# Seven block products in two of three d_ff groups of the gated expert for batches 0 and 1, the norm in its inputs, and a planner with one port for two engines

## The chip, the cores and the metric

One core of a Trainium2 chip runs the whole program. The metric is the device time of one execution in microseconds (us), given as the median of several runs. The engines are TensorE (PE, its weight load PEld), VectorE (DVE), ScalarE (ACT), GpSimd (POOL) and SyncE (SP, which only issues DMAs).

## The reference

The input is one attention layer (4 batches, 12 heads, 448 tokens, head size 64) and the weights of two dense layers behind it. Cut to what matters:

```
q_n, k_n = rmsnorm(q, g_q), rmsnorm(k, g_k)
x = softmax(q_n @ k_n.T / 8) @ v                     # to 1792 tokens x 768
h = x @ w_in;  y = elu(h) @ w_out                    # d_ff 2048
xn = y / sqrt(mean(y * y) + 1e-6) * rms_g
g = xn @ w_gate                                      # d_ff 1536
out = (g * sigmoid(g) * (xn @ w_val)) @ w_out2
```

All is float32. TensorE multiplies in a rounded form (fp32r), so each operand is split into a rounded high part and the difference, and a product of two 128-wide blocks takes three matmuls (high by high, high by low, low by high).

## The kernel before, in words

Everything is kept transposed: features on 128 partitions, the 448 tokens of one batch along the free side. 768 is 6 blocks, 2048 is 16 blocks, 1536 is 12 blocks. Attention goes by pairs of heads, 6 pairs to a batch, 24 in all; a pair is cut into 15 or 13 pieces (scores, softmax, transposes, product with v).

The work of the two dense layers stands in `STAGES` (line 558): the first layer for batch 0, the first for batch 1, the second for batches 0 and 1 together, the first for batches 2 and 3, the second for 2 and 3. They are called stages 1 to 5 here. `GOALS` (line 1308) says how many attention pairs are to be done by the end of each stage: 13.25, 19.75, then all 24. The main loop (line 1321 on) adds attention pieces between the steps of a stage at an even rate.

A stage goes by d_ff groups of four blocks (`NF1`, `NF2`): first the products into these four blocks, and then `acc_units` (line 1139), which multiplies them by the second matrix and adds to the result, six output blocks for each batch. In the second layer a group's first part is the gate and the value product of each block. There are three such groups.

Stages 1 to 3 are plain: `h_unit` and `gv_unit` (line 1242) make a block by `product` (line 1010) over six input blocks, 18 matmuls. Stages 4 and 5 (`FAST`, line 559) take two d_ff blocks and two batches at a time: `quad` (line 1024) gets four results by seven half-length products (`part`, three input blocks, 9 matmuls each) instead of eight. For that, `w_split` (line 612) makes the combinations of the weights (sa, sb) and `combo` (line 1048) those of the inputs: from B11, B21, B12, B22 it makes T1 to T4, and each of the seven names is split in high and low part. A set of inputs in that form fills 7 x 3 x 2 = 42 slots of `xslots`. There are 24 slots, and 18 more (`spare`) in buffers of the attention, which `late` (line 1311) adds once the last pair is done. At the end of stage 3 `combos` (line 1069) loads the spilled attention outputs of batches 2 and 3 and makes their 42 slots while TensorE does the last group's `acc_units`.

The rms norm of the second layer: `first_experts` (line 1166) puts rms_g into its output when it splits it (`y_done`, line 1172) and adds up squares; `norm` (line 1226) sums them over partitions by TensorE, takes the root on ACT and the reciprocal on DVE; the result rt is multiplied into the gate in `gv_unit` and `gv_quad` (line 1101), twice: once ahead of the tanh and once behind it.

Weights come as 768 KB chunks of six blocks. In its first use a chunk is converted to float32 by `w_convert` (line 630: two instructions on ACT or POOL, two on DVE) and, if used again, written back as `kept`; later stages load `kept`. Each is then split by `split_w` (line 603: a rounded copy, and a difference on DVE or POOL) into one of the four tiles of `r_w`; `late` adds two (`wide`).

The order of all instructions is made by `Plan` (line 34). Every operation is entered with the engines that can do it and a price on each (`copy`: DVE, ACT or POOL; `tt`: DVE or POOL; `stt`: DVE). `forward` (line 170) plays a list schedule with these prices, `backward` (line 131) makes ranks from it, and eight rounds of the two are made; the best order by its own reckoning is issued on every engine and DMA queue. An operation inside SBUF on DVE or POOL is made longer where the other engine runs too (`STRETCH`, 0.6 and 0.25 of the overlap). Buffers come in rings, and their reuse is a dependence: `r_m` has three product banks while attention runs (`phase`, line 548), `r_tp` six temporary tiles, eight after `late`.

Of the kernel before, what the change touches and what calls it, by code (L numbers as in the profile page):

```python
# [35 lines left out]
class Plan:  # L36
# [4 lines left out]
    PASSES = 8  # L41
    LAT = 0.2
# [6 lines left out]
    STRETCH = {"v": 0.6, "g": 0.25}  # L49
# [36 lines left out]
    def add(self, alts, outs, ins, lag=0.0, after=None, soon=False, dma=False):  # L86
# [24 lines left out]
        shared = not any(getattr(ap.tensor, "_space", None) == PSUM for ap in list(outs) + list(ins) if ap is not None)  # L111
        self.ops.append((alts, preds, lag, soon, dma, shared))

    def schedule(self):
# [5 lines left out]
        best, rank = None, list(range(n))  # L120
# [10 lines left out]
    def backward(self, span, start, eng, price, lat):  # L131
# [8 lines left out]
        def avail(i):  # L140
            e, is_dma = eng[i], self.ops[i][4]
            r = 0.0 if self.succ[i] else lat[i]
            for s in self.succ[i]:
                if is_dma:
                    gap = lat[i] + 0.1
                elif eng[s] == e:
                    gap = 0.06 if e != "pe" else 0.0
                else:
                    gap = lat[i] + self.LAT
                r = max(r, left[s] + gap)  # L150
            heapq.heappush(fut[e], (r, i))
# [18 lines left out]
    def forward(self, rank):  # L170
# [14 lines left out]
        port = {"v": 0.0, "g": 0.0}  # L185
# [3 lines left out]
        def avail(i):  # L189
            for e in self.ops[i][0]:  # L190
                r = 0.0
                for j in self.ops[i][1]:
                    if self.ops[j][4]:
                        f = done[j] + 0.1
                    elif eng[j] == e:
                        f = done[j] - self.ops[j][2] + (0.06 if e != "pe" else 0.0)
                    else:
                        f = done[j] + self.LAT
# [7 lines left out]
        while left:  # L206
# [23 lines left out]
            i = heapq.heappop(now[e])[1]  # L230
            alts = self.ops[i][0]
            back[e] -= alts[e][0]
            if taken[i]:
                continue
# [11 lines left out]
            if e in self.STRETCH and self.ops[i][5]:  # L246

                o = "g" if e == "v" else "v"
                price += self.STRETCH[e] * max(0.0, min(port[o], t + price) - t)
                port[e] = t + price  # L250
# [11 lines left out]
            else:  # L262
                done[i] = free[e] + self.ops[i][2]
# [31 lines left out]
def kernel(ctx: ExitStack, tc: tile.TileContext, dims, tok, qk, vr, gq, gk, wst, rmsg, ident_in, out):  # L295
# [42 lines left out]

    class Pair:
# [28 lines left out]
    def c_v1(n):  # L368
        return 0.15 + 0.00104 * n

    def c_v2(n):
        return 0.15 + 0.00052 * n

    def c_a(n):
        return 0.18 + 0.00083 * n

    def mm(o, l, r, start, stop, price=None):
        n = size(r)
        plan.add(
            {"pe": (price or max(0.108, n / 2400.0 + 0.017), lambda: T.matmul(o, l, r, start=start, stop=stop))},  # L380
            [o], [l, r] + ([] if start else [o]), lag=0.17,
        )

    def block(mms, price):
# [12 lines left out]
        plan.add({"pe": (price, go)}, list(outs.values()), list(ins.values()), lag=0.17)  # L397

    def transposes(pairs):
# [4 lines left out]
        plan.add({"pe": (0.02 + 0.11 * len(pairs), go)}, [o for o, _ in pairs], [i for _, i in pairs] + [ident], lag=0.17)  # L404

    def copy(dst, src, eng="vag"):
# [6 lines left out]
        if "a" in eng:  # L413
            alts["a"] = (c_a(n), lambda: A.activation(out=dst, in_=src, func=AF.Copy))
        if "g" in eng and not ps:
            alts["g"] = (
                0.2 + 0.00097 * n,
# [7 lines left out]
    def c_tt(a, b, n):  # L425
        return 0.2 + 0.0014 * n if two_sbuf(a, b) else c_v1(n)

    def tt(dst, a, b, op, eng="vg"):
# [4 lines left out]
        if "g" in eng and two_sbuf(a, b):  # L433
            alts["g"] = (0.25 + 0.0022 * n, lambda: G.tensor_tensor(out=dst, in0=a, in1=b, op=op))
# [18 lines left out]
    def act(dst, src, func, extra=0.0, accum=None, after=None, **kw):  # L453
        if accum is not None:
            kw["accum_out"] = accum
        plan.add(
            {"a": (c_a(size(src)) + extra, lambda: A.activation(out=dst, in_=src, func=func, **kw))},
# [3 lines left out]
    def vop(price, fn, outs, ins, after=None):  # L461
        plan.add({"v": (price, fn)}, outs, ins, after=after)

    def recip(dst, src):
        vop(0.15 + 0.00625 * size(dst), lambda: V.reciprocal(dst, src), [dst], [src])
# [30 lines left out]
    wraw = sb.tile([P, 2, 2 * WN], F32, name="wr")  # L496
    r_wr = Ring(tiles=[wraw[:, k].rearrange("p (n w) -> p n w", w=2) for k in range(2)])
    wf = wraw.rearrange("p a n -> p (a n)")
# [4 lines left out]
    tks = [tagged(1, [P, 15 * D], "tk")[0], wf[:, 0:15 * D]]  # L503
    tks += [yf[:, 7 * S:7 * S + 15 * D], yf[:, 12 * S - 15 * D:12 * S]]
    l_rw = Pair(tagged(1, [P, 1024], "rw")[0], wf[:, 1024:2048])
    l_rb = Pair(tagged(1, [P, 512], "rb")[0], wf[:, 2048:2560])
    l_qh = Pair(sb.tile([P, 1024], F32R, name="qh"), gf[:, 0:1024])
    l_ql = Pair(sb.tile([P, 1024], F32R, name="ql"), gf[:, 1024:2048])
    p_own = tagged(1, [P, 3, 2 * S], "p")[0]
    pt_own = tagged(1, [P, 2, 3, S], "pt")[0]  # L510
    l_p = Pair(p_own, tf[:, 0:6 * S].rearrange("p (a s) -> p a s", a=3))
    l_pj = Pair(tagged(1, [P, S], "pj")[0], tf[:, 6 * S:7 * S])
    l_pt = Pair(pt_own, yf[:, 0:6 * S].rearrange("p (h k s) -> p h k s", h=2, k=3))
    l_pe = Pair(tagged(1, [P, S], "pe")[0], yf[:, 6 * S:7 * S])
# [3 lines left out]
    r_sn = Ring("sn", 1, [P, NPB * 15])  # L518
# [11 lines left out]
    spare, wide = [], []  # L530
# [5 lines left out]
    for t in (l_rb.own, l_pj.own, l_pe.own, r_rv.t[0], r_rv.t[1], r_rsb.t[1]):  # L536
# [22 lines left out]
    FAST = (3, 4)  # L559
    OG = NF1 * CD // CW  # L560

    def steps_of(kind, fast):
        nums = list(one if kind == 1 else two)
        if not fast:
            return [("c", n) for n in nums]
# [871 lines left out]
```

## Time and profile before

| | us |
|---|---|
| median of 3 runs (1270.31 to 1271.68) | 1271.13 |
| the profiled execution | 1273.35 |
| its span, first to last instruction | 1271.6 |
| TensorE busy in the span (6300 matmuls) | 1231.3 |
| DVE, ACT, POOL busy | 835.1, 681.7, 919.1 |

The span is that of the profiled execution, which took 1273.35 us. Most of the program's instructions are recorded at line 319, since a wrapper issues them all, so groups go by tile names: bank is a PSUM bank, xs and late are input slots, w and late weight tiles, gbig the d_ff blocks, tbig, rsb and xf temporaries, ybig results, wr raw weights, wc converted ones. Matmul records overlap by their pipeline, so a busy time close to the length of a stretch doesn't say that the stretch is full; the count of matmuls in it says more.

### The profile page before, as it was taken

Reading aid. Unit: us, or ns where it says so; the run is one execution under the profiler, and the core shown is the slowest. Engines: PE = TensorE matmul, PEld = TensorE weight load, DVE = VectorE, ACT = ScalarE, POOL = GpSimd, SP = SyncE. Lnnn points to the kernel's source line nnn. Section 1 sums busy time; section 2 is a strip of 40 time slices with the busy share of each in tenths; the row PEclk is TensorE's granted clock in tenths of the full one; section 3 lists DMA queues with packets and bytes.
Section 4 is the critical chain, followed back from the end, with each engine's and each line's share of the span. In section 5 each row is a group of like instructions: output and inputs, shape, how many; then the busy total and the mean of one; then the engine's idle time right before and its main releaser. Section 6 shows DMA issues by size and latency. Waiting matters only on the chain.

```text
span 1271.6 us, 17832 instructions
## 1 busy us (share of the span) xinstructions
PE 1231.3 (97%) x6300; PEld 1025.9 (81%) x6300; DVE 835.1 (66%) x1276; ACT 681.7 (54%) x1328; POOL 919.1 (72%) x688
## 2 busy tenths in 40 slices
PE   4998999999999999999999999999999999999998
PEld 2556867777777877898988888999999978999997
DVE  6886888879545588764554547626354899486582
ACT  5876767676655577554554543535334754342240
POOL 3587879997766697775653569948476999798680
PEclk9998999999999999999999999999999999999999
DMA  5677676775443444664444435212121112122112
GB/s 201 190 227 260 245 247 234 240 248 156 165 131 120 124 178 160 218 202 161 156 165 128 149 94 169 88 38 75 47 66 63 38 32 73 58 63 75 38 50 87
DMA packets 62206, 173.44 MB, mean 136 GB/s; under 512 B 10654, under 2 KB 19876, under 8 KB 62116
## 3 DMA queue, kind: packets, MB, share of 16 engines
q1 hardware_dynamic: 53476, 163.31, 39.3%
q10 hardware_dynamic: 8640, 8.99, 2.5%
q8 instruction: 49, 0.80, 0.2%
q14 instruction: 41, 0.34, 0.1%
HBM read 137.11 MB, written 35.17 MB: 135 GB/s over the span
## 4 chain that ended last, share of the span: by engine, by line
PE 79%; POOL 9%; DVE 4%; DMA 3%; issue 2%; ACT 1%; SPq 0%; ACTq 0%; POOLq 0%; DVEq 0%
PE bank L319 79%; POOL w L319 2%; POOL tbig L319 1%; POOL gbig L319 1%; POOL late L319 1%; POOL wr L319 1%; POOL xs L319 1%; DVE bank L319 1%; DMA rb<-scr 1%; DVE ybig L319 1%; POOL ql L319 1%; DMA tk<-tok 0%; DMA ybig<-tok 0%; DMA wc<-kept 0%; DMA wr<-wst 0%
## 5 line engine op out<-in xcount | busy, mean ns | idle before, releaser
L319 PE MATMUL bank<-xs,w 128*128 128x448 f32 x1872 | 423.0, 371 | 1.7 <-DVE tbig L319 0.9
L319 PE MATMUL bank<-gbig,w 128*128 128x448 f32 x1872 | 408.0, 372 | 2.8 <-POOL gbig L319 2.7
L319 PEld LDWEIGHTS bank<-gbig,w 128*128 128x128 f32 x1872 | 347.8, 189 | 43.0 <-issue 7.1
L319 PEld LDWEIGHTS bank<-xs,w 128*128 128x128 f32 x1872 | 344.6, 188 | 38.2 <-issue 6.7
L319 POOL TENSOR_TENSOR w<-wc,w 128x768 fp32r<-128x768 f32 (+1 forms) x126 | 241.8, 1921 | 81.1 <-ACT w L319 75.1
L319 DVE TENSOR_REDUCE bank<-bank 128x1 f32<-128x448 f32 x168 | 99.3, 624 | 76.2 <-PE bank L319 75.8
L319 ACT ACTIVATE w<-wc 128x768 fp32r<-128x768 f32 (+1 forms) x82 | 65.2, 795 | 91.7 <-PE bank L319 85.8
L319 DVE SCALAR_TENSOR_TENSOR wc<-wc,wt 128x768 int32<-128x768 int32 x68 | 92.2, 1356 | 26.9 <-ACT wc L319 16.5
L319 POOL TENSOR_TENSOR gbig<-tbig,gbig 128x448 fp32r<-128x448 f32 x75 | 99.8, 1333 | 8.7 <-ACT gbig L319 7.4
L319 ACT ACTIVATE p<-bank,nm,rr 128x448 f32<-128x448 f32 x126 | 90.2, 720 | 27.2 <-DVE nm L319 20.6
L319 POOL TENSOR_SCALAR w<-wc 128x768 fp32r<-128x768 f32 x65 | 60.9, 938 | 57.5 <-PE bank L319 51.6
L319 ACT ACTIVATE pt<-bank 128x384 f32<-128x384 f32 (+1 forms) x161 | 68.7, 448 | 50.6 <-PE bank L319 47.8
L319 DVE TENSOR_TENSOR tbig<-bank,tbig 128x448 f32<-128x448 f32 x80 | 48.5, 617 | 57.5 <-PE bank L319 55.4
L319 POOL TENSOR_TENSOR tbig<-tbig 128x448 f32<-128x448 f32 x45 | 59.5, 1324 | 28.3 <-DVE tbig L319 27.1
L319 DVE TENSOR_TENSOR ybig<-bank,ybig 128x448 f32<-128x448 f32 x72 | 44.4, 619 | 49.0 <-PE bank L319 48.8
L319 PE MATMUL bank<-ident,p 128*128 128x128 f32 x441 | 70.6, 277 | 5.4 <-ACT p L319 3.7
L319 PEld LDWEIGHTS bank<-ident,p 128*128 128x128 f32 x441 | 53.8, 141 | 23.0 <-ACT p L319 4.3
L319 PE MATMUL bank<-xs,late 128*128 128x448 f32 x288 | 69.5, 370 | 0.4 <-DVE xs L319 0.4
L319 DVE TENSOR_SCALAR wt<-wr 128x768 uint16<-128x768 uint16 x68 | 67.7, 995 | 1.5 <-DMA wr<-wst 1.2
L319 DVE SCALAR_TENSOR_TENSOR ybig<-bank,ybig 128x448 f32<-128x448 f32 x48 | 29.8, 622 | 55.1 <-PE bank L319 55.1
L319 PE MATMUL bank<-late,w 128*128 128x448 f32 x252 | 64.6, 368 | 0.0
L319 ACT ACTIVATE wt<-wr 128x768 uint16<-128x768 uint8 x42 | 45.7, 1089 | 28.6 <-DVE wc L319 20.7
(232 smaller groups left out, 2105.1 us busy)
## 6 DMA issues: line engine op xcount, KB each, us to landing
wr<-wst SPq DMA_DIRECT2D x68, 768.0 KB
wc<-kept SPq DMA_DIRECT2D x100, 384.0 KB
kept<-wc SPq DMA_DIRECT2D x68, 384.0 KB
rw<-qk SPq DMA_DIRECT2D x21, 512.0 KB
tk<-tok SPq DMA_DIRECT2D x20, 480.0 KB
rv<-vr SPq DMA_DIRECT2D x24, 256.0 KB
out_t<-ybig SPq DMA_DIRECT2D x24, 224.0 KB
rb<-scr ACTq DMA_DIRECT2D x36, 128.0 KB
```

The source lines that it names most:

```text
L319: return lambda *a, **k: f(*[real(x) for x in a], **{n: real(x) for n, x in k.items()})
```

## The change

Of the three d_ff groups of stage 3, the first stays plain and the other two go by quads (`PLAIN`). For that the norm factor is multiplied into the inputs of batches 0 and 1 (`scale`, right behind `norm`), with a copy of the scaled block written to DRAM; `gv_unit` and `gv_quad` for these batches no longer use rt. Between the first group's products and its `acc_units`, the loop finishes attention, adds the spare slots and calls `widen`, which loads the scaled blocks again and makes T1 to T4; the splits of B11, B21 and B22 are there already. The two wide weight tiles are now the raw weight tiles, and come at the end of stage 3. The second-stage goal is 20.25 pairs, and the rest of attention is spread over the first group's eight units of stage 3. Some buffers change places: wr, p and pt become separate tiles, and pe is 512 wide, so that one copy fills both its halves in `t_bank`.

The planner has new prices, 22 rounds from ranks with noise, and one port: an operation of POOL, and one of DVE inside SBUF, begins only when the other's is over, and DVE may take another ready operation that doesn't need the port.

```diff
-    PASSES = 8
-    LAT = 0.2
+    PASSES = 22
+    SEED = 17
+    HOP = {"pe": 0.12, "v": 0.04, "a": 0.04, "g": 0.09, "sp": 0.04}
+    TAIL = {"pe": 0.0, "v": 0.085, "a": 0.11, "g": 0.04, "sp": 0.0}
+    BEHIND = {"v": 0.15, "g": 0.05}
+    SLACK = 0.1
-    STRETCH = {"v": 0.6, "g": 0.25}
...
-        best, rank = None, list(range(n))
+        noise = random.Random(self.SEED)
+        best, rank = None, [i + 40 * noise.random() for i in range(n)]
...
+            if e == "v" and self.ops[i][5] and port > t + 0.1:
+                x = min((x for x in now["v"] if not taken[x[1]] and not self.ops[x[1]][5] and t + self.ops[x[1]][0]["v"][0] <= port + self.SLACK), default=None)
...
-            if e in self.STRETCH and self.ops[i][5]:
-
-                o = "g" if e == "v" else "v"
-                price += self.STRETCH[e] * max(0.0, min(port[o], t + price) - t)
-                port[e] = t + price
+            if e == "g" or e == "v" and self.ops[i][5]:
+                if port > t:
+                    price = port - t + max(0.03, price - self.BEHIND[e])
+                port = t + price + self.TAIL[e]
...
     def c_v1(n):
-        return 0.15 + 0.00104 * n
+        return 0.064 + 0.00105 * n
...
+    def c_gt(n):
+        return 0.14 + 0.00216 * n
...
     def c_tt(a, b, n):
-        return 0.2 + 0.0014 * n if two_sbuf(a, b) else c_v1(n)
+        return c_v1(n)
...
-            alts["g"] = (0.25 + 0.0022 * n, lambda: G.tensor_tensor(out=dst, in0=a, in1=b, op=op))
+            alts["g"] = (c_gt(n), lambda: G.tensor_tensor(out=dst, in0=a, in1=b, op=op))
...
-    for t in (p_own, pt_own):
+    for t, k in ((p_own[2], 2), (pt_own[1], 3)):
         f = again(t)
-        wide.append(f[:, 0:2 * WN].rearrange("p (a n) -> p a n", a=2))
-        spare += [f[:, 2 * WN + k * S:2 * WN + (k + 1) * S] for k in range(2)]
-    r_ws = Ring(tiles=[wf[:, k * WN:(k + 1) * WN] for k in range(2)])
-    r_th = Ring(tiles=[wf[:, 2 * WN + k * S:2 * WN + (k + 1) * S] for k in range(3)] + [r_wt.t[0][:, 0:S]])
+        spare += [f[:, j * S:(j + 1) * S] for j in range(k)]
+    wide = [again(t).rearrange("p (a n) -> p a n", a=2) for t in wr]
+    r_ws = Ring(tiles=[t[:, 0:WN] for t in p_own[0:2]])
+    r_th = Ring(tiles=[pt_own[0][:, k] for k in range(3)] + [l_pj.own])
...
-    FAST = (3, 4)
+    PLAIN = (9, 9, 1, 0, 0)
...
-            copy(pe[0:64, 64:S], ps[0:64, 0:M3], "va")
-            copy(pe[64:128, 0:M3], ps[64:128, 0:M3], "va")
+            copy(pe[:, 64:S], ps[:, 0:M3], "va")
...
-    def combo(c, x):
+    def combo(c, x, ready={}):
         def sp(name, t):
-            h, l = xslots.get(), xslots.get()
-            copy(h, t)
-            tt(l, t, h, ALU.subtract)
+            if name in ready:
+                h, l = ready[name]
+            else:
+                h, l = xslots.get(), xslots.get()
+                copy(h, t)
+                tt(l, t, h, ALU.subtract)
...
         def gate(i, j, o):
-            u, th = r_tp.next(), r_th.next()
+            th = ths[i, j] = r_th.next()
+            if bs[j] < 2:
+                act(th, o, AF.Tanh, scale=0.5)
+                stt(th, th, 1.0, o, ALU.add, ALU.mult)
+                return
+            u = r_tp.next()
...
+    def widen(bs):
+        b0, b1 = bs
+        for c in range(3):
+            x = [r_tp.next() for _ in range(4)]
+            for t, (b, k) in zip(x, ((b0, c), (b0, c + 3), (b1, c), (b1, c + 3))):
+                dma(t, xsp[b, k], P * S * 4)
+            done = {n: xns[b][k] for n, b, k in (("B11", b0, c), ("B21", b0, c + 3), ("B22", b1, c + 3))}
+            combo(c, x, done)
...
-            if not fast:
-                xh, xl = xslots.get(), xslots.get()
-                act(xh, ye, AF.Copy, scale=g)
-                stt(xl, ye, g, xh, ALU.mult, ALU.subtract)
-                xns[b][e] = (xh, xl)
...
+            if not fast:
+                xns[b][e] = ye
+                return
...
+    def scale(b):
+        for e in E_ORDER:
+            ye = xns[b][e]
+            stt(ye, ye, rg[:, e:e + 1], rt[b], ALU.mult, ALU.mult)
+            xh, xl = xslots.get(), xslots.get()
+            copy(xh, ye)
+            tt(xl, ye, xh, ALU.subtract)
+            xns[b][e] = (xh, xl)
+            xsp[b, e] = tc.dram_tile([P, S], F32, name=f"xsp{b}_{e}")
+            dma(xsp[b, e], ye, P * S * 4)
+            yslots.put(ye)
...
-            u, th = r_tp.next(), r_tp.next()
-            tt(u, og, rt[b], ALU.mult)
-            act(th, u, AF.Tanh, scale=0.5)
-            stt(th, th, 1.0, u, ALU.add, ALU.mult)
-            tt(th, th, rt[b], ALU.mult)
-            ths[b] = th
+            th = ths[b] = r_tp.next()
+            act(th, og, AF.Tanh, scale=0.5)
+            stt(th, th, 1.0, og, ALU.add, ALU.mult)
...
+        fast = f0 >= plain * NF2
...
+            if f0 + NF2 == plain * NF2:
+                for x in xns[bs[1]][0:3]:
+                    for z in x:
+                        xslots.put(z)
+                yield "late"
+                widen(bs)
             yield from acc_units(bs, f0, NF2, f0 == 0, last, ob, True, o_done)
+            if f0 + NF2 == plain * NF2:
+                phase(2)
...
-    GOALS = [13.25, 19.75, 24, 24, 24]
+    GOALS = [13.25, 20.25, 24, 24, 24]
...
             for b in bs:
                 norm(b)
+                if b < 2:
+                    scale(b)
```

## Rows read from the trace of the kernel before

**Rows 1.** The page, parts 1 and 2: busy time by engine, TensorE's 40 slices.

```profile
PE 1231.3 (97%) x6300; PEld 1025.9 (81%) x6300; DVE 835.1 (66%) x1276; ACT 681.7 (54%) x1328; POOL 919.1 (72%) x688
...
PE   4998999999999999999999999999999999999998
```

**Rows 2.** Windows: stretch, length, busy us (count) by engine, granted clock, DMA share, GB/s.

```profile
0.00:30.00 30.00, 12.64 (x62) 8.25 (x62) 19.64 (x52) 15.85 (x29) 7.87 (x13) 1.00 0.60 212
...
90.00:120.00 30.00, 25.73 (x131) 18.83 (x130) 20.35 (x27) 17.14 (x28) 22.04 (x18) 0.99 0.82 275
120.00:150.00 30.00, 29.21 (x142) 23.73 (x142) 23.02 (x33) 21.67 (x44) 25.76 (x18) 0.90 0.73 248
...
270.00:300.00 30.00, 28.18 (x148) 22.30 (x149) 24.98 (x38) 18.09 (x34) 24.44 (x18) 1.00 0.68 210
...
1020.00:1050.00 30.00, 27.70 (x123) 22.99 (x122) 29.82 (x28) 16.47 (x27) 30.00 (x21) 0.94 0.13 40
...
1110.00:1140.00 30.00, 30.00 (x149) 27.57 (x148) 25.43 (x33) 12.61 (x20) 28.36 (x20) 1.00 0.17 54
1140.00:1170.00 30.00, 30.00 (x147) 27.36 (x146) 22.13 (x30) 10.93 (x17) 27.16 (x19) 1.00 0.26 80
...
560.00:765.00 205.00, 204.97 (x1055) 175.14 (x1053) 100.21 (x159) 104.58 (x184) 112.22 (x85) 1.00 0.45 146
```

**Rows 3.** Waits of TensorE, longest first: total us, times, longest us.

```profile
PE bank L319 <- DVE rr L319: 8.0, 1, 8.0
```

**Rows 4.** Timeline of TensorE, end of stage 3: start, us, group, idle before it.

```profile
765.03 29.44 PE L319 MATMUL bank<-gbig,w 128*128 128x448 f32 x144
...
799.17 1.28 PE L319 MATMUL bank<-late,late 128*128 128x448 f32 x5 [0.23 <-POOL late L319]
```

**Rows 5.** Timeline, stage 3's first products and batch 1's reciprocal.

```profile
477.08 0.89 PE L319 MATMUL bank<-xs,w 128*128 128x448 f32 x3
...
488.31 2.94 DVE L319 RECIPROCAL tbig<-tbig 128x448 f32<-128x448 f32 x1
```

**Rows 6.** Timeline, single instructions of DVE and POOL inside SBUF.

```profile
455.62 0.96 DVE L319 TENSOR_TENSOR w<-wc,w 128x768 fp32r<-128x768 f32 x1 [0.38 <-ACT w L319]
...
483.81 0.60 DVE L319 TENSOR_TENSOR gbig<-tbig,gbig 128x448 fp32r<-128x448 f32 x1
...
484.34 0.60 DVE L319 TENSOR_SCALAR wt<-wr 128x768 uint16<-128x768 uint16 x1
...
487.45 0.95 DVE L319 SCALAR_TENSOR_TENSOR wc<-wc,wt 128x768 int32<-128x768 int32 x1
...
490.61 1.84 POOL L319 TENSOR_TENSOR w<-wc,w 128x768 fp32r<-128x768 f32 x1
...
491.17 1.74 DVE L319 TENSOR_SCALAR wt<-wr 128x768 uint16<-128x768 uint16 x1
...
772.53 0.56 DVE L319 TENSOR_TENSOR wr<-wc 128x384 f32<-128x384 f32 x1 [0.21 <-DMA wc<-kept]
...
783.35 1.01 POOL L319 TENSOR_TENSOR wr<-wc,wc 128x384 f32<-128x384 f32 x1
```

**Rows 7.** Groups by form: count, busy us, mean ns, idle before and its releasers.

```profile
L319 POOL TENSOR_TENSOR w<-wc,w 128x768 fp32r<-128x768 f32 x117 | 230.6, 1972 | 80.3 <-ACT w L319 74.3 <-PE bank L319 2.5
...
L319 DVE TENSOR_TENSOR tbig<-bank,tbig 128x448 f32<-128x448 f32 x80 | 48.5, 617 | 57.5 <-PE bank L319 55.4 <-ACT tbig L319 1.6 <-issue 0.2
...
L319 DVE TENSOR_TENSOR w<-wc,w 128x768 fp32r<-128x768 f32 x19 | 27.6, 1453 | 4.8 <-ACT w L319 3.0 <-POOL w L319 1.8
```

**Rows 8.** Windows, instructions on the xs slots alone, columns as in rows 2.

```profile
477.00:493.80 16.80, 9.98 (x42) 7.51 (x42) 4.05 (x4) 1.33 (x2) 0.00 (x0) 1.00 0.34 112
```

**Rows 9.** Timeline, first and last instruction of the inputs for batches 2, 3.

```profile
755.20 0.58 ACT L319 ACTIVATE xs<-tbig 128x448 fp32r<-128x448 f32 x1
...
802.74 1.15 POOL L319 TENSOR_TENSOR late<-tbig,late 128x448 fp32r<-128x448 f32 x1 [0.69 <-ACT late L319]
```

**Rows 10.** Windows, the last second-matrix products of stage 3, columns as in rows 2.

```profile
765.00:794.50 29.50, 29.50 (x147) 27.34 (x146) 21.98 (x26) 9.07 (x17) 28.17 (x22) 1.00 0.59 174
```

More of the change, by code (lines that the diff above doesn't have):

```diff
@@ L84, in region, with add @@
         return ap.name, halves, m
-    def add(self, alts, outs, ins, lag=0.0, after=None, soon=False, dma=False):
+    def add(self, alts, outs, ins, lag=0.0, after=None, soon=False, dma=False, port=True):
         i = len(self.ops)
@@ L110, in add @@
                 self.hist[name] = keep
-        shared = not any(getattr(ap.tensor, "_space", None) == PSUM for ap in list(outs) + list(ins) if ap is not None)
+        shared = port and not any(getattr(ap.tensor, "_space", None) == PSUM for ap in list(outs) + list(ins) if ap is not None)
         self.ops.append((alts, preds, lag, soon, dma, shared))
@@ L337, in next, with grow @@
             return self.t[(self.k - 1) % len(self.t)]
+        def grow(self, more):
+            j = self.k % len(self.t)
+            self.t = list(more) + self.t[j:] + self.t[:j]
+            self.k = 0
     class Pair:
@@ L402, in go @@
                 T.transpose(o, i, ident)
-        plan.add({"pe": (0.02 + 0.11 * len(pairs), go)}, [o for o, _ in pairs], [i for _, i in pairs] + [ident], lag=0.17)
+        plan.add({"pe": (0.02 + 0.11 * len(pairs), go)}, [o for o, _ in pairs], [i for _, i in pairs] + [ident], lag=0.16)
     def copy(dst, src, eng="vag"):
@@ L455, in act, with vop @@
             kw["accum_out"] = accum
+            extra += 0.09
+        if any(hasattr(kw.get(k), "tensor") for k in ("scale", "bias")):
+            extra += 0.09
         plan.add(
-            {"a": (c_a(size(src)) + extra, lambda: A.activation(out=dst, in_=src, func=func, **kw))},
+            {"a": (c_a(size(src), in_psum(src)) + extra, lambda: A.activation(out=dst, in_=src, func=func, **kw))},
             [dst, accum], [src] + [x for x in kw.values() if hasattr(x, "tensor") and x is not accum], after=after,
         )
-    def vop(price, fn, outs, ins, after=None):
-        plan.add({"v": (price, fn)}, outs, ins, after=after)
+    def vop(price, fn, outs, ins, after=None, port=False):
+        plan.add({"v": (price, fn)}, outs, ins, after=after, port=port)
     def recip(dst, src):
-        vop(0.15 + 0.00625 * size(dst), lambda: V.reciprocal(dst, src), [dst], [src])
+        vop(0.1 + 0.00625 * size(dst), lambda: V.reciprocal(dst, src), [dst], [src])
     def dma(dst, src, nbytes, after=None, soon=False, by="sp"):
@@ L495 @@
     WN = CW * P
-    wraw = sb.tile([P, 2, 2 * WN], F32, name="wr")
-    r_wr = Ring(tiles=[wraw[:, k].rearrange("p (n w) -> p n w", w=2) for k in range(2)])
-    wf = wraw.rearrange("p a n -> p (a n)")
+    wr = tagged(2, [P, 2 * WN], "wr")
+    r_wr = Ring(tiles=[t.rearrange("p (n w) -> p n w", w=2) for t in wr])
     r_wc = Ring("wc", 3, [P, WN])
@@ L568, in steps_of @@
         for g in range(len(nums) // (nf + OG)):
+            if g < plain:
+                res += [("c", n) for n in nums[k:k + nf + OG]]
+                k += nf + OG
+                continue
             if kind == 1:
@@ L577, in steps_of @@
         return res
-    stream = [st for s, (kind, _) in enumerate(STAGES) for st in steps_of(kind, s in FAST)]
+    stream = [st for s, (kind, _) in enumerate(STAGES) for st in steps_of(kind, PLAIN[s])]
     spl_w = {}
@@ L1323 @@
         ahead = STAGES[s + 1] if s + 1 < len(STAGES) else None
-        spilled = ahead is not None and ahead[0] == 1 and ahead[1][0] >= 2
-        count = UNITS[kind] - (CD if spilled else 0)
-        rate = max(goal - pieces["n"], 0) / count
+        count = UNITS[kind] if kind == 1 else 2 * NF2 * PLAIN[s]
+        rate = max(goal - pieces["n"], 0) / max(count, 1)
         credit = 0.0
-        if s and GOALS[s - 1] >= NPAIR:
-            until(target(NPAIR) + 1)
-            phase(2)
         if kind == 2:
@@ L1334 @@
                     norm(b)
-        for step in (first_experts if kind == 1 else second_experts)(bs, s in FAST):
+        for step in first_experts(bs, s >= 3) if kind == 1 else second_experts(bs, PLAIN[s]):
+            if step == "late":
+                until(target(NPAIR) + 1)
+                late()
+                continue
             if step == "next":
-                if ahead is not None and ahead[0] == 1 and s + 1 in FAST:
-                    if not state:
-                        until(target(NPAIR) + 1)
-                        late()
+                if ahead is not None and ahead[0] == 1 and s + 1 >= 3:
+                    r_w.grow(wide)
                     combos(ahead[1])
```

130 lines of the change are left out of this document (62 added, 68 removed).

## The prediction

> **What bounds the kernel now.** The page's summary comes first: TensorE is busy for 1231.3 of 1271.6 us, the others 54 to 72%, and the slices keep TensorE at 9 from the third on [rows 1]. So a microsecond counts only if it leaves or enters TensorE's stream. Busy time hides small gaps, so I read the 30 us windows next, where the reader should compare the count of matmuls too [rows 2]. Full windows of quad products hold 147 to 149; the poor ones are those of the start (12.64 us busy of 30), of 90 to 150 us (25.73 busy in one, 0.90 of the granted clock in the other), of 270 to 300, and 1020 to 1050, with 123 matmuls where DVE and POOL are both busy all the time (29.82 and 30.00). Stage 3, which the change rewrites, is none of these: from 560 to 765 us TensorE is busy 204.97 of 205 us. The list of waits says the same: its longest, 8.0 us, belongs to the start [rows 3]. In stage 3 there is nothing to gain but matmuls.
>
> **Matmuls removed.** In one d_ff group of four blocks, plain gate and val cost 4 blocks x 2 matrices x 2 batches x 18 = 288 matmuls; four quads cost 4 x 7 x 9 = 252. Two groups change: 72 matmuls go. The second-matrix products of a group are 144 matmuls in 29.44 us [rows 4], 0.2044 us each. 72 x 0.2044 = **-14.7 us**, all on the path.
>
> **Norm moved ahead of stage 3.** Before, g alone is put into the inputs, and rt into the gate's outputs, so stage 3's products start at 477.08 while batch 1's norm is under way: the reciprocal runs from 488.31 to 491.25 [rows 5]. After, batch 1's first input needs that reciprocal, then the scaling, the rounding copy and the difference (about 0.6 each on a free DVE or ACT, 1.15 on POOL [rows 6, 9]): about 493.8. Queued behind it are six such inputs, and their spill writes on SP. Until then TensorE has batch 0's gate and val of one block, 36 matmuls, since the three product banks rotate and the next waits for batch 1; attention stays as it was. In 477 to 493.8 it ran 42 matmuls on xs [rows 8], so 6 (1.2 us) lack. Ends: 0, if the new ranks pull the chain forward, and 1.2 plus five more inputs at 1.5 us, 8.7. I take **+2**, near the low end, because 3.75 pairs of attention are still there to fill. Batch 0's norm has all of stage 2 as cover: nothing.
>
> **The T operands between groups 0 and 1.** widen makes 4 combinations and 4 splits for each of three c: 36 instructions (24 two-input, 12 copies) and 12 loads. It needs attention's buffers and batch 1's first inputs, so it waits for the last attention pair and the last plain product; its cover is group 0's 29.44 us of second-matrix products. The nearest thing in the trace is the same job for batches 2, 3: 54 such instructions, from 755.20 to 803.89, beside an equal 29.44 us, with a wait of 0.23 us at its end [rows 4, 9]. There DVE is busy 21.98 and POOL 28.17 of 29.5 us [rows 10], with no weight conversion in it. Now there are 18 fewer of these but six chunks to convert: 6 x (0.60 + 0.95) = 9.3 us of DVE [rows 6]. Ends: 0 (two thirds of the work) and 9.3, all of it uncovered. I take **+3**, a third, as the 18 left out (9 copies, and 9 differences at 1.15 on POOL) give 10.4 us of POOL back. The last group's own step to batches 2, 3 begins a few us later, since all 42 slots are held until the last quad; the same 0.23 us wait says that it just fits: inside these ends.
>
> **The quads themselves.** Per two quads (126 matmuls, 25.7 us of TensorE), unstretched durations [rows 6, 7, 9]: DVE reading PSUM 20 x 0.62 = 12.4; DVE inside SBUF, fixed, 4 chunks x (0.60 + 0.95) + 0.6 = 6.8; movable between DVE and POOL 8 half sums, 6 full and 2 half weight differences, 5 others, 14.4 on DVE (at 0.56, 0.96, 0.60) or 26.9 on POOL (1.01, 1.84, 1.15). The rows show that SBUF work of the two goes one after the other: a DVE instruction of 0.60 us, issued at 491.17 beside a POOL difference that ends at 492.45, takes 1.74 us and ends at 492.91 [rows 6]. With a share x of the movable on DVE, DVE needs 19.2 + 14.4x and the two in SBUF 33.7 - 12.5x; they meet at x = 0.54, 27.0 us, 1.3 over TensorE, 5.2 for four such pairs. Stage 5's quads by the same sum (no conversion, two rt products more per gate) need 25.6, and there 149 and 147 matmuls per 30 us run without a gap [rows 2]. So the new quads are some 5% past a load that was just carried, and a quad's weights prefetched under each group's second-matrix products take part of it. Ends 0 and 5.2 at the best split; I take **+2**. Dropped with rt: two instructions per gate and batch, off the path.
>
> By the Trainium skill (SBUF — State Buffer, Who interferes with whom) the pair of ports that VectorE and GpSimd share is an exclusive lock, held for the whole instruction. The row at 491.17 agrees; by the partial stretch that the old plan assumed (0.6 and 0.25) the two quads would need about 22 us and cost 0, by the rule 5.2.
>
> **Attention squeezed.** The last 3.75 pairs now sit in 8 units instead of 30-odd. Eight units of 36 matmuls are 58.9 us of products, 15.7 to a pair; stage 1 had 576 matmuls, 117.7 us, for 7.25 pairs, 16.2 to one. So it is stage 1's density, where a worse window (270 to 300) leaves TensorE idle for 1.8 us [rows 2]. Against that 0.5 pair moves to stage 2, which has room. I count 0 here, since the waits above already hold it.
>
> **The new plan.** All orders change: 22 passes from noisy ranks, new prices, a lock in place of stretches. Open to it are the idle times after the first 30 us: 90 to 150, 270 to 300 and 1020 to 1050 alone hold 4.3 + 0.8 + 1.8 + 23 missing matmuls (4.7) = 11.6 us [rows 2], more with the stretches like them between. A new order can lose as well. Ends -18 and +5. I take **-6**, half of the 11.6: the worst of it (1020 to 1050) is two engines contending, which the new model prices.
>
> **Sum.** -14.7 + 2 + 3 + 2 - 6 = -13.7. The profiled execution took 1273.35 us (span 1271.6); so 1259.65, and as the median of runs, 1271.13, lies 2.2 lower, **1257.4 us**.
>
> **Rivals.** *The new waits eat the gain:* norm 4, T operands 5, quads 4, plan only -3: -4.7, 1266.4. For: every engine is loaded just there. Against: 560 to 765 us has DVE at 100 of 205 us, room to work ahead. *The plan opens more:* it takes the -18 and stage 3 costs 7: -25.7, 1245.4. For: 11.6 us are visible; against: most of the rest is start-up chains over DMA. *Slower, by the port:* if the plan leaves the movable work on POOL, as it does now (117 weight differences there [rows 7], 19 on DVE in the same form), the SBUF sum per two quads is 33.7 - 12.5x. It decides once it passes 25.7 + 14.7/4 = 29.4, at x below 0.34; at x = 0.2 it is 31.2, 5.5 over, +22 in all: -14.7 + 22 + 2 + 3 - 6 = +6.3, 1277.4. Against: the old prices called DVE's difference 1.28 us for 768 columns, the new one 0.87, so work moves to DVE. That the change does nothing is out: the 72 matmuls are in the program or not.
>
> **Chances.** Forecast 0.50 (1250 to 1263), waits eating the gain 0.24 (1263 to 1271, its last bit no change), plan opening more 0.15 (1240 to 1250), port 0.11. A measurement here can tell about 0.2%, 2.5 us: faster 0.82, within it 0.07, slower 0.11. The range 1245 to 1270 leaves out the port case, and the ends of two others, about 0.2.
>
> **What would show it.** Right: 6228 matmuls; TensorE dense in the quads of stage 3, a gap of a few us or none before batch 1's first product, DVE's SBUF differences more and POOL's fewer, 1020 to 1050 fuller. Wrong: TensorE waiting on POOL w, POOL or DVE tbig in stage 3's quads (port), on xs after the reciprocal (norm), or on late tiles after group 0 (T operands) for over 5 us each; or new gaps in stages 1 and 2, where the change removes no work.

## The result, and the profile after

The changed kernel takes 1238.55 us against 1270.72 us for the one before on the same chip: ratio 0.974 (95% interval 0.9721 to 0.976), 32 us faster; one of its four executions, at 3015.5 us, was in a slow state and is left out of the ratio. The forecast was 1257.4, with a range from 1245 to 1270. The sign was right; the forecast gain of 13.7 us was less than half of the measured one. Run again beside other kernels in a later job, it took 1238.10 us (0.9744, 0.9725 to 0.9762).

The profiled execution took 1236.46 us. The page's parts 1 and 2, to be read against [rows 1]:

```profile
span 1234.7 us, 17825 instructions
...
PE 1201.6 (97%) x6228; PEld 1009.7 (82%) x6228; DVE 883.5 (72%) x1332; ACT 720.9 (58%) x1413; POOL 903.7 (73%) x651
...
PE   3999999999999999999999999999999989999998
```

TensorE runs 6228 matmuls, 72 fewer, as counted. Its idle time outside those busy 1201.6 us went from 40.3 to 33.1 us, and busy time itself fell by 29.7 us, twice the removed matmuls' 14.7. Gaps too short to show as idle, stretches at a lower granted clock (0.90 to 0.94 in [rows 2]) and the slower rhythm of the last section all count as busy. So the windows' counts have to be read. First those of the changed kernel, one long stretch and six short ones (columns as in [rows 2]):

```profile
30.00:330.00 300.00, 295.32 (x1625) 217.45 (x1625) 244.19 (x429) 242.73 (x536) 224.43 (x164) 0.99 0.71 234
...
600.00:630.00 30.00, 30.00 (x149) 27.69 (x148) 25.20 (x30) 18.68 (x29) 28.30 (x20) 1.00 0.39 134
630.00:660.00 30.00, 30.00 (x149) 27.69 (x149) 27.66 (x36) 17.42 (x25) 28.20 (x19) 1.00 0.42 152
...
690.00:720.00 30.00, 30.00 (x150) 27.79 (x149) 29.33 (x36) 18.03 (x27) 28.17 (x20) 1.00 0.47 165
720.00:750.00 30.00, 30.00 (x150) 27.80 (x149) 29.87 (x35) 18.84 (x31) 29.11 (x20) 1.00 0.54 179
...
990.00:1020.00 30.00, 25.96 (x119) 21.34 (x117) 29.55 (x28) 13.55 (x21) 29.44 (x22) 1.00 0.17 53
1020.00:1050.00 30.00, 29.61 (x147) 27.38 (x147) 29.46 (x45) 12.12 (x20) 26.01 (x18) 1.00 0.24 68
```

The same long stretch of the kernel before:

```profile
30.00:330.00 300.00, 284.27 (x1521) 207.09 (x1522) 248.14 (x418) 216.98 (x467) 246.36 (x183) 0.98 0.69 226
```

Three things are to be seen. In the first 330 us, where the change takes away no matmul, TensorE is busy for 11 us more and gets 104 matmuls further. In stage 3's quads (600 to 780 us) it runs 149 to 150 per 30 us and waits for nothing, though in the fullest of these windows (720 to 750) DVE is busy for 29.87 and POOL for 29.11 of 30 us. And the step from stage 4 to stage 5 (990 to 1020, [rows 2] had it at 1020 to 1050) is as poor as it was: 119 matmuls.

The span can be cut into three parts. Up to stage 3's first product the changed kernel:

```profile
0.00:468.84 468.84, 443.71 (x2443) 330.20 (x2444) 343.44 (x637) 349.83 (x770) 320.53 (x241) 0.99 0.64 211
```

and the kernel before:

```profile
0.00:477.08 477.08, 443.99 (x2397) 328.77 (x2397) 350.92 (x631) 322.15 (x708) 355.11 (x277) 0.99 0.61 197
```

Stage 3 begins 8.2 us earlier with 46 more matmuls done, attention that used to come later. At this stretch's 0.192 us per matmul they are some 8.8 us, so the start gained about 17 us. From there to the last 2273 matmuls, which are stages 4 and 5 in both kernels, it takes 293.7 in place of 317.2 us. Less the 8.8 us of moved attention, that is 14.7, the price of the 72 matmuls. The last 2273 take 472.2 in place of 477.3 us. These are estimates from one profiled execution of each kernel; the two spans are 36.9 us apart, the medians 32.

### The profile page after: what moved, and what is told of

Same layout as the page of the kernel before. It is cut to its first block, busy times and chain, and to the rows that moved or that the text cites. A ratio compares the mean times of both kernels' runs of the same rounds, so it can differ in the third digit from the quotient of the medians.

```text
span 1234.7 us, 17825 instructions
## 1 busy us (share of the span) xinstructions
PE 1201.6 (97%) x6228; PEld 1009.7 (82%) x6228; DVE 883.5 (72%) x1332; ACT 720.9 (58%) x1413; POOL 903.7 (73%) x651
## 4 chain that ended last, share of the span: by engine, by line
PE 88%; DVE 5%; ACT 2%; DMA 2%; issue 1%; POOL 1%; SPq 0%; ACTq 0%; DVEq 0%
PE bank L331 88%; DVE tbig L331 2%; DMA wr<-wst 1%; DVE rw L331 1%; ACT tbig L331 1%; DVE w L331 1%; DMA ybig<-tok 0%; DMA rb<-scr 0%; ACT p L331 0%; DVE bank L331 0%; POOL w L331 0%; DVE ybig L331 0%; DVE ss L331 0%; DVE ql L331 0%; DMA wc<-kept 0%
## 5 line engine op out<-in xcount | busy, mean ns | idle before, releaser
L331 PE MATMUL bank<-xs,w 128*128 128x448 f32 x1584 | 364.5, 371 | 1.8 <-DVE tbig L331 1.1
L331 PEld LDWEIGHTS bank<-xs,w 128*128 128x128 f32 x1584 | 290.6, 188 | 31.9 <-issue 7.1
L331 POOL TENSOR_TENSOR w<-wc,w 128x768 fp32r<-128x768 f32 (+1 forms) x120 | 226.8, 1892 | 54.4 <-ACT w L331 48.2
L331 PE MATMUL bank<-late,w 128*128 128x448 f32 x420 | 100.6, 366 | 0.8 <-DVE w L331 0.8
L331 ACT ACTIVATE pt<-bank 128x384 f32<-128x384 f32 (+2 forms) x175 | 75.7, 451 | 22.9 <-PE bank L331 20.6
L331 POOL TENSOR_TENSOR gbig<-tbig,gbig 128x448 fp32r<-128x448 f32 x57 | 76.9, 1354 | 13.5 <-ACT gbig L331 12.8
L331 PEld LDWEIGHTS bank<-late,w 128*128 128x128 f32 x420 | 78.8, 188 | 7.7 <-DVE w L331 1.2
L331 POOL TENSOR_TENSOR w<-p,w 128x768 fp32r<-128x768 f32 x32 | 64.5, 2017 | 20.2 <-ACT w L331 19.7
L331 POOL TENSOR_SCALAR w<-wc 128x768 fp32r<-128x768 f32 (+1 forms) x48 | 45.4, 947 | 44.4 <-PE bank L331 35.1
L331 ACT ACTIVATE tbig<-bank 128x448 f32<-128x448 f32 x78 | 42.1, 541 | 39.8 <-PE bank L331 31.9
```

The costliest lines, as they stand in the source:

```text
L331: return lambda *a, **k: f(*[real(x) for x in a], **{n: real(x) for n, x in k.items()})
```

## The experiments

All were timed in three rounds beside the kernel before, whose median lay between 1269.80 and 1270.82 us in these jobs. They answer five questions in turn.

**1. Is it the planner or the work?** plan_only is the kernel before with the new class Plan and the new prices alone; work_only is the changed kernel with the old ones.

```diff
 # plan_only: before.py, and of the change only this and the prices it uses
+    PASSES = 22
+    SEED = 17
...
+            if e == "g" or e == "v" and self.ops[i][5]:
+                if port > t:
 # work_only: the changed kernel, and this and the old prices back
+    PASSES = 8
+    STRETCH = {"v": 0.6, "g": 0.25}
```

> The work, buffers and goals of before, ordered by the new planner (prices, port, 22 noisy rounds). Theory A (the planner gave most of what the forecast missed): TensorE's gaps of the first 330 us go from some 38 us to under 12 as in the changed kernel, time 1249 to 1254 us (17 to 22 below before). Theory B (the gain beyond the matmuls comes from the work: norm in the inputs, attention squeezed, separate buffers): at most 6 below, 1264 to 1269.

Measured: 1265.48 us (0.996, 0.9944 to 0.9976), 4 below before. That is B's side.

> The changed work, buffers and goals, ordered by the old planner with its old prices and partial stretch. A: 72 matmuls are 14.7 us, the new waits of stage 3 (forecast: 7) show up here, so 1257 to 1264 us. B: most of the 32 us is kept, 1240 to 1246. If the old planner can't feed the quads at all (the port rival of the forecast): 1271 or more, with TensorE waiting on POOL's weight differences between 600 and 780 us.

Measured: 1262.48 us (0.994, 0.992 to 0.9959), 7 below before: A's side. Neither part gives the 32 us, and the two together, 12, fall far short of it. Both theories fall as they were put (the expectation for seed_101 below calls the two that are left C and D): either single orders differ by more than I had allowed, or the parts need each other. The next two changes of the planner and three of its noise ask for that.

```diff
 # search_back: the changed kernel
-    PASSES = 22
+    PASSES = 8
-        best, rank = None, [i + 40 * noise.random() for i in range(n)]
+        best, rank = None, list(range(n))
 # search_only: work_only
-    PASSES = 8
+    PASSES = 22
-        best, rank = None, list(range(n))
+        best, rank = None, [i + 40 * noise.random() for i in range(n)]
 # port_back: the changed kernel, new prices and search, with the old partial stretch (cut: DVE's choice of another operation while the port is taken goes too)
-            if e == "g" or e == "v" and self.ops[i][5]:
-                if port > t:
-                    price = port - t + max(0.03, price - self.BEHIND[e])
-                port = t + price + self.TAIL[e]
+            if e in self.STRETCH and self.ops[i][5]:
+                o = "g" if e == "v" else "v"
+                price += self.STRETCH[e] * max(0.0, min(port[o], t + price) - t)
+                port[e] = t + price
```

> The changed kernel with the new prices and the port, but the old search: 8 rounds from ranks without noise. If search gives little: 1238 to 1244. If the better search is a main part of the gain (rival): over 1248, with gaps mainly in stages 1 and 2.

Measured: 1250.10 us (0.9853, 0.9829 to 0.9877): 12 above seed 17, and 5 to 8 above the other three seeds below. It is one order, so the search's own share can't be told from the spread of orders. Its stage 3 is dense (240.00 us busy from 570 to 810); it loses before (1576 matmuls from 30 to 330 us, against 1625).

> The changed work with the old prices, the old hop time and the old partial stretch, but 22 rounds from noisy ranks. If search is the gain: under 1250 us. If the picture of the engines (prices, hops, port) is: 1255 to 1262, at most 6 below work_only's 1262.5.

Measured: 1255.36 us (0.9886, 0.9866 to 0.9906). Search gives the old picture 7 us too, just past the 6 expected. With the same search and seed the changed kernel is 17 us faster, so the picture of the engines counts for more than the search here, in one order of each.

> The changed kernel, its planner with the new prices and 22 noisy rounds, but with the old partial stretch in place of the exclusive port. If the port model is what the new plan gains by: 6 us or more above the changed kernel (over 1244), with DVE and POOL waiting longer and TensorE gaps in stage 1 and in the quads of stage 3. If it is prices and search alone: within 2 us of it (1236 to 1241).

Measured: 1312.03 us (1.0318, 1.0296 to 1.034), 73 us above the changed kernel. The list of waits of TensorE in port_back (total us, times, longest):

```profile
PE bank L325 <- POOL gbig L325: 13.0, 14, 4.2
PE bank L325 <- DVE rs L325: 10.7, 6, 4.4
PE bank L325 <- POOL rsb L325: 7.8, 1, 7.8
```

With the low new prices and no exclusive port the planner believes in two engines that run beside each other, and TensorE waits on POOL's and DVE's results. The old planner had the same partial stretch, but prices so high (0.2 + 0.0014 n for a DVE difference of n columns) that they may have covered part of the waiting. At 73 us, five times the widest spread of orders below, the port has to be in this model once the prices are honest. By the Trainium skill (SBUF — State Buffer, Who interferes with whom) whichever of the two engines issues first holds the shared pair of ports for the whole instruction, and the other blocks; the row at 491.17 [rows 6] shows it on one instruction. This run shows only what a plan without it costs here.

**2. How much does one order differ from another?**

```diff
 # seed_101, seed_107, seed_250: the changed kernel; plan_only_101, plan_only_107: plan_only
-    SEED = 17
+    SEED = 101
```

> The changed kernel with other noise in its first ranks (seed 101). Theory C (work and planner both matter, and a good part of the 19 us that neither part alone gives is one lucky order): 1242 to 1250 us, with gaps in stages 1 and 2 of 5 to 10 us more. Theory D (new planner and new work need each other: the quads load DVE and POOL so far that only a planner that knows the port can feed them): 1236 to 1241, the same as seed 17.

> The same with a third noise (seed 107). C: it differs from seed 17 and from seed 101 by several us, 1242 to 1252. D: within 3 us of seed 17.

> The changed kernel with the noise that gives the shortest schedule by the planner's own reckoning among 123 seeds (0.4 us under seed 17's). If the reckoning picks orders that are fast on the chip: 1236 to 1241, level with seed 17 and 3 us or more below seeds 101 and 107. If what differs on the chip is outside its reckoning: anywhere from 1238 to 1248.

Measured: 1243.81 (0.9791, 0.9777 to 0.9806), 1245.01 (0.9795, 0.9779 to 0.9812) and 1242.27 us (0.9794, 0.9766 to 0.9821). Seed 17 is the best of four by 4 to 6 us: theory C for that much. The order that is shortest by the planner's own reckoning (seed 250) is level with seeds 101 and 107 within the intervals, and not with 17: what sets the last 4 us is outside its reckoning, or nearly.

> The kernel before with the new planner, seed 107 in place of 17. If planner alone is worth about 5 us on the old work whatever the noise: 1260 to 1268. If 1265.5 was an unlucky order: under 1257.

> The kernel before with the new planner, seed 101. Planner alone with other noise gave 1265.5 and 1251.9. If it is worth about 11 us with an order's own spread of some 6: 1252 to 1266. Over 1267: the planner is worth little, and seed 107 was the lucky one.

Measured: 1251.90 (0.9863, 0.9845 to 0.9881) and 1261.67 us (0.9931, 0.9911 to 0.9952). With 1265.48 that is a mean of 1259.7 over three orders, 11 below before, and a spread of 13.6 us. plan_only's seed 17 is the worst of the three orders of the old work and the best of the new one, which is part of why the first two runs did not add up. In means, the planner's 11 and the 7 of work_only still leave 10 of the 28 us between the kernel before (1270.2) and the four orders of the new one (1242.4). The old planner gave one order for each work, so whether these 10 are its poor orders or the two parts needing each other (theory D) is not shown. The gain of a good order lies in the first stages. The stretch from 30 to 330 us of plan_only:

```profile
30.00:330.00 300.00, 288.84 (x1558) 209.27 (x1559) 239.69 (x421) 239.56 (x525) 212.27 (x162) 0.98 0.68 227
```

and of plan_only_107:

```profile
30.00:330.00 300.00, 297.79 (x1616) 217.78 (x1616) 242.20 (x418) 244.55 (x533) 225.24 (x166) 1.00 0.69 232
```

Between them 58 matmuls and 9 us of busy time in the first 330 us make most of the 13.6 us.

> The kernel before with the new planner and the changed buffers (wr, p and pt as separate tiles, pe 512 wide and filled by one copy, small temporaries), without norm in the inputs, quads in stage 3, and goals. If the buffers are what the planner alone lacked: 8 us or more below planner alone (1265.5), under 1258. If not, within 3 us of it.

plan_buffers is plan_only with the changed tiles. Its edit, in short:

```diff
-    wraw = sb.tile([P, 2, 2 * WN], F32, name="wr")
+    wr = tagged(2, [P, 2 * WN], "wr")
...
-    p_own = tagged(1, [P, 3, 2 * S], "p")[0]
+    p_own = tagged(3, [P, 2 * S], "p")
...
+            copy(pe[:, 64:S], ps[:, 0:M3], "va")
```

Measured: 1269.88 us (0.999, 0.9976 to 1.0005). No gain from the buffers can be seen; it is one order more, 4 us above the worst of plan_only. Counted as a fourth order of the old work it makes the planner's mean gain 8 in place of 11 us.

**3. What are the quads worth?** no_quads keeps the norm in the inputs, with three plain groups in stage 3; the rest of attention then spreads over the units of all three.

```diff
-    PLAIN = (9, 9, 1, 0, 0)
+    PLAIN = (9, 9, 3, 0, 0)
...
-            if f0 + NF2 == plain * NF2:
-                for x in xns[bs[1]][0:3]:
-                    for z in x:
-                        xslots.put(z)
-                yield "late"
-                widen(bs)
```

> The changed kernel with all three groups of stage 3 plain again (norm still in the inputs, no T operands there, attention spread over all 24 units). If the quads of stage 3 cost no wait: 14.7 us above the changed kernel, about 1253 us. If they cost the 5 us (T operands and quads) of the forecast: only 9 to 10 above, 1248. A gap of TensorE before batch 1's first input shows the price of the norm.

> no_quads with seed 101. If stage 3's quads cost no waits: 14.7 us above seed_101's 1243.8 in the mean of the orders, so 1254 to 1264.

Measured: 1259.84 (0.9919, 0.9902 to 0.9936) and 1261.30 us (0.9924, 0.9904 to 0.9944). Their mean, 1260.6, is 18 us above the mean of the four orders of the changed kernel (1242.4): 14.7 us of matmuls, no waits, and 3.5 that are within the spread of orders. The first run's expectation, about 1253, missed by 7 us, since it was reckoned from seed 17.

**4. What is the norm's place worth?** norm_back keeps the quads. g alone goes into the inputs, and rt into the gates.

```diff
-            if bs[j] < 2:
-                act(th, o, AF.Tanh, scale=0.5)
-                stt(th, th, 1.0, o, ALU.add, ALU.mult)
-                return
...
             if not fast:
-                xns[b][e] = ye
+                act(ye, ye, AF.Copy, scale=g)
+                xh, xl = xslots.get(), xslots.get()
...
-                if b < 2:
-                    scale(b)
```

> The changed kernel with the norm where it was: g alone in the inputs of batches 0 and 1 (split, spilled and combined without it), rt again multiplied into the gate twice. If the forecast's norm step was right (a wait of 2 us at stage 3's start, and two products per gate off the path): 2 us faster than the changed kernel or within the 6 us that another order costs, 1236 to 1245. If taking 64 products out of the loaded quads and units is what lets stage 3 run dense (rival): 1247 to 1257, with TensorE gaps between 600 and 780 us.

> norm_back with seed 101. If the rt products overload the quads of stage 3 in any order: 10 us or more of TensorE gaps between 570 and 810 us again, on w tiles, and 1256 to 1266. If that was one bad order: under 1250, with no such gaps.

Measured: 1262.09 (0.9941, 0.9921 to 0.9961) and 1259.26 us (0.9907, 0.9889 to 0.9926): the rival, the first run 5 us past its range. In means, the old work under the new planner takes 1259.7, the norm in the inputs without quads 1260.6, quads without that norm 1260.7, and both together 1242.4 us. Neither half gives anything alone; together they give 17 us (plan_only also has the old buffers and goals). Where, the windows say. norm_back from 570 to 810 us, then two of its short windows:

```profile
570.00:810.00 240.00, 230.18 (x1107) 206.55 (x1106) 209.62 (x240) 131.11 (x202) 216.25 (x143) 0.98 0.44 148
...
630.00:660.00 30.00, 26.03 (x120) 23.24 (x119) 28.85 (x34) 16.63 (x24) 28.14 (x19) 0.94 0.28 98
...
720.00:750.00 30.00, 27.21 (x124) 24.09 (x122) 28.87 (x38) 14.79 (x23) 27.41 (x18) 0.94 0.37 118
```

norm_back_101, the same 240 us:

```profile
570.00:810.00 240.00, 234.19 (x1139) 210.98 (x1138) 214.51 (x245) 134.42 (x207) 226.47 (x149) 0.99 0.46 153
```

and the changed kernel:

```profile
570.00:810.00 240.00, 240.00 (x1182) 219.53 (x1181) 198.50 (x225) 132.46 (x205) 219.71 (x150) 1.00 0.46 156
```

75 and 43 matmuls fewer at some 0.203 us are 15 and 9 us lost in these quads, in either order, while DVE works 11 to 16 us more. Cut by counts as above, stage 3 takes 310.9 and 302.9 us, and 293.7 to 295.9 in the changed kernel's four orders. The waits of TensorE in that stretch of norm_back are on weights:

```profile
PE bank L331 <- ACT w L331: 4.5, 3, 2.1
PE bank L331 <- POOL w L331: 3.5, 2, 2.0
PE bank L331 <- DVE w L331: 1.2, 2, 1.0
```

In norm_back_101 they add up to 5.8 us, 4.6 of them on weights, under the 10 expected. That the weight splits come late because DVE and POOL also have the gates' products to do is the likely reason; only the waits are shown. The changed kernel has no wait of TensorE at all between 470 and 810 us. Its granted clock is 1.00 there; in norm_back's windows with gaps the mean is 0.94, so part of them ran at the lower level, and from 720 to 750 us the loss (26 matmuls, 5.3 us) is larger than TensorE's idle time there, 2.8 us.

**5. Does the result hold?** The changed kernel once more.

```diff
 # after_again: the changed kernel, nothing edited
```

> The changed kernel itself once more, beside the others on this chip: 1236 to 1241, and TensorE's gaps at the same places.

Measured: 1238.10 us (0.9744, 0.9725 to 0.9762). No run beat it.

## Why the prediction was wrong

Its terms, with means over orders: the planner on the old work gives -10.5 (1270.2 to 1259.7, three orders); the new work on the new planner -17.3 (1259.7 to 1242.4, four orders); the one order that was put into the kernel another -3.9. Together -31.7. The forecast was -13.7. Of the 18 us between, the planner makes 8.4 (-6 against -14.4 with its seed), the waits 7 (+7 against 0), and 2.6 are what the new work gave beyond its matmuls, within the spread of orders. The split depends on the order of counting: on the new work, against work_only, the planner measures -20, and the work under the old planner -7. The seed's 3.9 us are luck; the mean of four orders, 1242.4, lies below the range without it.

- **Matmuls, -14.7: right.** 72 fewer, and no_quads shows 18 between means, orders included. It takes the norm in the inputs to get them: norm_back has the same 72 fewer, and no gain.
- **Norm ahead of stage 3, +2: wrong, 0 as a wait.** Stage 3 began at 468.84 us, and batch 1's reciprocal 8.2 us later, 3 us sooner than before ([rows 5]: 11.2); attention (480.11) and batch 0's products filled the rest. The changed kernel's timeline of TensorE and DVE there:

```profile
468.84 0.77 PE L331 MATMUL bank<-xs,w 128*128 128x448 f32 x3
...
472.21 0.66 PE L331 MATMUL bank<-gbig,ones 128*128 128x448 f32 x2
...
477.07 2.94 DVE L331 RECIPROCAL tbig<-tbig 128x448 f32<-128x448 f32 x1
...
480.11 2.48 PE L331 MATMUL bank<-pt,rv 128*64 128x448 f32 x12
...
483.82 3.29 PE L331 MATMUL bank<-xs,w 128*128 128x448 f32 x15
```

  Of that step the low end held. What failed as an explanation, though no term of the sum hung on it, is a sentence on the quads: "Dropped with rt: two instructions per gate and batch, off the path." In the quads those instructions are the path, and taking them out is worth 9 to 15 us there. The forecast's own arithmetic points there. With rt back, three more gate steps on DVE have both inputs in SBUF (1.8 us) and five more products are movable (3.0 us on DVE, 5.75 on POOL): DVE needs 21.0 + 17.4x, the two in SBUF 41.3 - 15.3x, 31.8 us per two quads, 6 over TensorE in place of 1.3. I worked that sum for stage 5, where no weights are converted, and not for stage 3 with rt, the case that the change avoids. As an absolute limit the sum doesn't hold (see the quads below); as a difference it does better. Between 570 and 810 us DVE makes 6 of 41 weight differences of 768 columns in the changed kernel, and 14 of 39 and 13 of 40 in norm_back's two orders. With these shares as x (0.15 and 0.35) the sums are 31.8 and 35.9 us, 4 apart, 16 for the four pairs of quads, near the 9 to 15 that were lost.
- **T operands, +3: wrong, 0.** No wait of TensorE between 470 and 810 us. Loads began at 518 us, and the last splits slid into the first quad, whose later parts alone need them. The changed kernel's timeline, SP's first load, TensorE around the first quad's start, and POOL's last difference:

```profile
518.07 0.32 SPq L331 DMA_DIRECT2D tbig<-xsp  x1
...
595.65 3.81 PE L331 MATMUL bank<-gbig,w 128*128 128x448 f32 x18
599.29 0.77 PE L331 MATMUL bank<-xs,w 128*128 128x448 f32 x3
599.91 2.59 PE L331 MATMUL bank<-gbig,w 128*128 128x448 f32 x12
...
608.27 1.16 POOL L331 TENSOR_TENSOR late<-xf,late 128x448 fp32r<-128x448 f32 x1 [0.69 <-ACT late L331]
```

  The cover was counted as the 29.44 us of second-matrix products; it is longer by the parts that don't need the last T.
- **Quads, +2: wrong, 0**, and not by the mechanism foretold. The sum took x = 0.54, since the new prices would move work to DVE. They did not. The weight differences of 768 columns in the changed kernel, 570 to 810 us:

```profile
L331 POOL TENSOR_TENSOR w<-wc,w 128x768 fp32r<-128x768 f32 x18 | 36.4, 2022 | 3.0 <-ACT w L331 2.9
L331 POOL TENSOR_TENSOR w<-p,w 128x768 fp32r<-128x768 f32 x17 | 34.9, 2060 | 2.0 <-ACT w L331 1.9
...
L331 DVE TENSOR_TENSOR w<-wc,w 128x768 fp32r<-128x768 f32 x4 | 7.2, 1808 | 0.2 <-POOL w L331 0.2
...
L331 DVE TENSOR_TENSOR w<-p,w 128x768 fp32r<-128x768 f32 x2 | 2.5, 1266 | 0.0
```

  At their x of 0.15 the sum is 31.8 us per two quads, 6 over TensorE, and TensorE waited for nothing. So the sum per two quads is no limit by itself. Part of it is not paid: the DVE instruction at 491.17 [rows 6] needs 0.46 us behind POOL's and not its free 0.60. And part is done ahead: from 653 to 682 us, under second-matrix products, two of the quads' combined weights are split (w<-p,w on POOL). How the 6 us divide was not measured. DVE's 29.87 of 30 us are not all work either, for its four differences w<-wc,w take 1808 ns in the mean where 0.96 us is the free duration. Conversions and rt together were too much, conversions alone were not. The 22 us given for the old plan's partial stretch leave that stretch out; with DVE's SBUF work wholly beside POOL's it is some 26.6 us by the same rows, close to the 27.0.
- **New plan, -6: the step that failed, mis-sized most.** It measured -10.5 in the mean of three orders, -4 and -18 at their ends (so the mean itself is good to some 4 us), and in the changed kernel 4 more for its seed. The forecast took half of the idle time seen in four windows, and put its hope on 1020 to 1050 us; that stretch got no better (119 matmuls against 123). The gain came from 30 to 330 us (104 matmuls further), of which it had counted 6.9 us (90 to 150 and 270 to 300) and put down most of the rest to "start-up chains over DMA". The rival with the plan opening more (1245.4) had the mechanism: its -18 is near the 14 us of planner and seed, but it still charged 7 us for stage 3.
- **The port rival and the rival of new waits** did not happen in the changed kernel, though the port rival's condition, x below 0.34, did. port_back shows what a planner without the port costs (+73), norm_back shows waits that eat the gain.

What stays open: why one order is 4 us faster on the chip than another that the planner reckons as good. Most of it is there before stage 3, whose first product comes at 468.84 us with seed 17 and at 473.17, 475.68 and 473.29 with seeds 101, 107 and 250, with equally much attention done.

## What to carry to other kernels

When a stage is at the limit of two side engines, work out their load with and without each small operation that a change removes; there an operation "off the path" can be the path. Try the parts of a change singly and together: here each of two gave nothing alone, and both gave 17 us. If a list scheduler orders the kernel, its picture of the engines is part of the kernel: honest prices need the shared port with them (73 us here). And before an edit of some per cent is judged by one schedule, time three or four orders of both versions, for here one order differs from another by up to 13.6 us.

## What the runs showed of the hardware that was not expected

Back-to-back matmuls of 448 columns run in one of two steady rhythms at a granted clock of 1.00, with 206.7 or 202.7 ns from start to start in the mean of 144, and an order can stay in the slower one for tens of us. The timeline of TensorE before, 144 products of one group, and three blocks in front of them with their starts 0.62 us apart:

```profile
818.63 0.78 PE L319 MATMUL bank<-xs,late 128*128 128x448 f32 x3
819.25 0.78 PE L319 MATMUL bank<-ql,late 128*128 128x448 f32 x3
819.87 0.78 PE L319 MATMUL bank<-late,late 128*128 128x448 f32 x3
820.49 29.92 PE L319 MATMUL bank<-gbig,w 128*128 128x448 f32 x144
```

and the changed kernel's, with 0.61 us between blocks:

```profile
651.83 0.77 PE L331 MATMUL bank<-late,w 128*128 128x448 f32 x3
652.43 0.77 PE L331 MATMUL bank<-xs,w 128*128 128x448 f32 x3
653.04 29.35 PE L331 MATMUL bank<-gbig,w 128*128 128x448 f32 x144
```

The same 144 matmuls take 29.92 or 29.35 us, without a wait in either. The kernel before has both: its group at 765.03 [rows 4] took 29.44 us. The old planner is not the cause by itself, for in work_only such a group at 676.72 takes 29.35 us. Over dense stretches of 120 us it is 585 matmuls before (840 to 960 us) and 593 after (600 to 720 us):

```profile
840.00:960.00 120.00, 120.00 (x585) 109.49 (x584) 53.27 (x76) 43.71 (x74) 73.84 (x56) 1.00 0.19 56
```

```profile
600.00:720.00 120.00, 120.00 (x593) 110.97 (x592) 101.26 (x126) 67.54 (x96) 107.74 (x73) 1.00 0.48 170
```

That is 1.4%, in stretches where TensorE is busy throughout. The changed kernel spends less of its time in the slow rhythm, which may be most of the 5 us by which its last 2273 matmuls are faster. What sets the rhythm was not tried.
